# A Fourier mixing layer with a gated product: the inverse's butterflies leave VectorE, two products of a step trade places, and a slot moves

## The chip, the cores and the metric

The kernel runs on one core of a Trainium2 chip. The metric is device time in microseconds, the median of three executions. The five engines run their own queues in order: PE (TensorE, matmuls), DVE (VectorE), ACT (ScalarE), POOL (GpSimd) and SP (which issues DMAs). An instruction that waits holds up all behind it on its engine.

## What is computed

For 8 batches of 3072 tokens of 256 features: a Fourier transform along the tokens, a complex 256 x 256 mixing with bias, a soft threshold, the inverse transform, and on its real output y a gated product of three weight matrices:

```
X  = rfft(x, axis=1)
Yr = Xr @ w_r - Xi @ w_i + b_r ;  Yi = Xr @ w_i + Xi @ w_r + b_i
Y  = soft(Yr) + 1j * soft(Yi)        # sign(a) * max(|a| - 0.01, 0)
y  = irfft(Y, n=3072, axis=1)
out = ((y @ w_a) * (y @ w_b)) @ w_out   # 256 -> 1536 -> 256
```

## The kernel before

The tokens are cut into 32 pairs of blocks (4 pairs a batch, 2 x 384 tokens each). The gated product of a pair runs in 12 steps, one for each 128 columns of the 1536, so there are 384 steps in a row; they are named pair.step here (5.3 is step 3 of pair 5). The step is in `step`. The two products with w_a and w_b are done as seven products of 384 columns, `run(0)` to `run(5)` in the step itself and a seventh, run(6), in `last_prod` one step later. Each is split into high and low parts, so each is three matmuls: ych with the low weight (wcNl), ych with the high one (wcNh), ycl with the high one. The result of a step, g, is multiplied with w_out in four pieces, `proj` 0 to 3, one step later; a piece too is three matmuls (0 and 1 of 256 columns, 2 and 3 of 512).

A step works in two of the PSUM banks X (bank_75 and bank_76 by turns) and in ya (bank_77) and yb (bank_78). ACT copies X after run(0) (the copy s1) and after run(2) (s2), and yb after run(3) (s5), since the next product is added on top or a later operation needs the part alone. run(2) needs s1 done, run(4) needs s5, run(5) needs s2. After run(4) a chain of four makes g from yb: two DVE products, a cast on ACT, a subtraction on DVE; run(3) of the next step needs yb, proj 0 and 1 need g. After run(5) DVE adds X to s5, and run(6) needs that. After run(6) a chain of three makes the other half of g, for proj 2 and 3.

Between the products a step has two slots. `slot()` takes a task from a list: a piece of the transform of the next batch. f1 is the first stage; f2 reads gs (sums on POOL); f3 has two halves, of which the second ends with four reads of its bank by DVE (the tile zy); i1 is the inverse's first stage, stored to d_d. All tasks share one bank, bank_79, so a task waits until the one before has been read.

The inverse's last stage is done by no matmul but by sums and scalings in SBUF: `idft` loads a tile wk from d_d and does some thirty operations on it in one chain, the last four of which write y. `yr_sums` follows with three sums of y on DVE, `yr_split` with the high and low parts (ych on ACT, ycl on POOL or DVE), into a ring. All this must be there when the next pair starts; in the last step of a pair, `yr_have` puts out whatever is missing, ahead of the rest of the step.

The order of the instructions on each engine is made by the class `Order`, a planner that keeps its own clock (`pe`, moved on by each matmul) and for each engine the time at which it comes free. `chain` gives it operations, each with the engines that may take it (G is POOL, V DVE, A ACT). Urgent ones go out when they are ready; `lazy` ones when they could start by now; `spare` ones after the lazy ones. Between two operations on different engines it reckons `HOP` = 165 ns. While `hold` is set, lazy and spare operations on ACT that would end after it are kept back. `need` puts a chain out and moves the planner's clock to its end, `vacate` the same for a bank.

Of the kernel before, what the change touches and what calls it, by code (L numbers as in the profile page):

```python
# [15 lines left out]
ALU = mybir.AluOpType  # L16

B, S, D, DFF = 8, 3072, 256, 1536
# [191 lines left out]
class Order:  # L210
# [35 lines left out]
    def chain(self, *ops, urgent=0, spare=False, after=0.0):  # L246

        c = {"ops": deque(ops), "left": len(ops), "n": len(ops), "times": [(max(self.pe + self.FROM, after), None)], "urgent": urgent}  # L250
        if urgent:
            self._push(c)
        else:
            (self.spare if spare else self.lazy).append(c)
        return c

    def _ready(self, c, engine=None):
        op = c["ops"][0]
        back = min(op[3] if len(op) > 3 else 1, len(c["times"]))
        t, e = c["times"][-back]  # L260
        return t if e is None else t + (self.same if e == (engine or op[0][0].upper()) else self.HOP)
# [99 lines left out]
def fft_mix_glu_kernel(ctx: ExitStack, tc: tile.TileContext, x, w_r, w_i, b_r, b_i, w_a, w_b, w_out, c1f, vf, m2, t2, c3, b1, m2b, vb, out):  # L361
# [24 lines left out]
    def tt(e, o, a, b, op):  # L386
        (nc.vector if e == "V" else nc.gpsimd).tensor_tensor(o, a, b, op=op)  # L387
# [675 lines left out]
    C3, C8, T8 = math.sqrt(0.75), math.cos(math.pi / 8), math.tan(math.pi / 8)  # L1063
    HALF = math.sqrt(0.5)

    def idft(b, q, wait=False):
# [14 lines left out]
        def size(*dims):  # L1081
            return math.prod(n for _, n in dims) * (1 if dims[-1][0] == 1 else 16)

        def add(o, x, y, op=ALU.add, engines="GV", back=1):
            n = size(*o[1:])
            o, x, y = (z if isinstance(z, bass.AP) else at(*z) for z in (o, x, y))
            ops.append((engines, n, lambda e: tt(e, o, x, y, op), back))

        def sub(o, x, y, **kw):
            add(o, x, y, ALU.subtract, **kw)  # L1090
# [6 lines left out]
        def mul_add(o, x, f, y, op=ALU.add):  # L1097
            n = size(*o[1:])
            o, x, y = at(*o), at(*x), at(*y)
            ops.append(("V", n, lambda e: nc.vector.scalar_tensor_tensor(o, x, f, y, op0=ALU.mult, op1=op)))  # L1100

        rows, flat = ((W, 4), (1, P)), ((1, 512),)
        x = [(A + P * i, *rows) for i in range(3)]
        sub((T, (P, 4), (1, P)), x[1], x[2])
# [3 lines left out]
        mul_add(x[2], x[1], -0.5, x[0])  # L1108
        add(x[0], x[0], x[1])
        turn = (640, (P, 4), (1, P))  # L1110
# [6 lines left out]
        for r, f in ((slice(0, 3, 2), C8), (slice(1, 2), HALF)):  # L1117
            v = (T2 + 192 * r.start, (384, 2), (1, 192)) if r.start == 0 else (T2 + 192, (1, 192))
            scale(v, v, f)
        o = [[(T2 + 192 * r + 16 * c, (32, 6)) for c in range(2)] for r in range(3)]  # L1120
        w = [[(A + 192 * r + 16 * c, (32, 6)) for c in range(2)] for r in range(3)]
        mul_add(w[0][0], o[0][1], T8, o[0][0])
        mul_add(w[0][1], o[0][0], -T8, o[0][1])
        mul_add(w[2][0], o[2][0], T8, o[2][1], ALU.subtract)
        mul_add(w[2][1], o[2][1], T8, o[2][0])
# [29 lines left out]
        for th in range(2):  # L1155
            for pq in range(2):
# [3 lines left out]
                ops.append(("GV", W, last))  # L1160
        yr["idft"] = od.chain(*ops, ("S", 0, lambda e: yr_sums(p)), after=ready)
# [125 lines left out]
    def step(n, nxt):  # L1287
# [27 lines left out]
        od.vacate(X)  # L1315
        run(0, X, True)
# [15 lines left out]
        od.need(c1_)  # L1332
        run(2, X)
# [5 lines left out]
        if not (tasks and tasks[0]):  # L1339
            od.hold = od.pe + 3 * (W / 2.4 + 2.8) + od.FROM  # L1340
# [5 lines left out]
        proj(pp, pj, 0)  # L1346
        slot()
        if n == 0:
            busy(3, *unread)
        proj(pp, pj, 1)  # L1350
        od.need(c5_)
        od.hold = None
# [15 lines left out]
        od.need(c2_)  # L1368
        run(5, X)
        od.put(c5_)  # L1370
        held[p, j] = X, s5, od.chain(add(s5, X), urgent=1)
        for i in range(2, 4):
            proj(pp, pj, i)
# [229 lines left out]
```

## Time and profile before

| | us |
|---|---|
| median of 3 executions (lowest, highest) | 2836.59 (2834.68, 2836.78) |
| the profiled execution | 2837.05 |
| its span, first to last instruction | 2835.3 |
| PE busy | 2792.2 (98%) |
| DVE busy | 2006.7 (71%) |
| ACT busy | 1397.7 (49%) |
| POOL busy | 1300.4 (46%) |
| mean granted clock of PE | 0.999 of full speed |

Matmuls overlap in the profile: the next one starts 0.17 us after a 384-column one whose own row says 0.34. So a busy PE can still lose time, and the distance from start to start tells more than the busy share. A product of three without a wait takes 0.52 us.

### The profile page before, as it was taken

What the parts mean: (1) busy time and instruction counts of PE and PEld (TensorE: products, weight loads), DVE (VectorE), ACT (ScalarE), POOL (GpSimd) and SP (SyncE); (2) the same over time, 40 slices, a digit from 0 to 9 for tenths busy, and PEclk for the clock granted to TensorE, in tenths of its full rate; (3) what the DMA queues carried; (4) which work ended last, traced back from release to release, by engine and by line L of the source; (5) the groups of instructions that cost most, each with busy time, mean ns of one, the idle gap of its engine ahead of it and who ended that gap; (6) DMA issues with size and microseconds to landing.
All of it is one profiled execution on the core that took longest, in us unless ns stands there. A gap on an engine that the chain in (4) does not pass through costs nothing.

```text
span 2835.3 us, 46772 instructions
## 1 busy us (share of the span) xinstructions
PE 2792.2 (98%) x16375; PEld 2605.7 (92%) x16375; DVE 2006.7 (71%) x3801; ACT 1397.7 (49%) x3059; POOL 1300.4 (46%) x1466
## 2 busy tenths in 40 slices
PE   9999999999999999999999999999999999999999
PEld 6799998999999999999999999999999999999998
DVE  4876667777677776777766777668677677666665
ACT  4654445544455444644446444464444544444443
POOL 1233336456364453654545644356544566343330
PEclk9999999999999999999999999999999999999999
DMA  8531113212132111321113121131211322110000
GB/s 248 169 101 48 54 53 100 82 44 62 54 93 71 57 49 50 100 69 56 48 46 114 60 68 33 59 105 54 68 36 56 109 62 67 37 39 21 22 8 23
DMA packets 157056, 190.91 MB, mean 67 GB/s; under 512 B 28344, under 2 KB 117300, under 8 KB 156740
## 3 DMA queue, kind: packets, MB, share of 16 engines
q1 hardware_dynamic: 154620, 180.12, 20.7%
q0 software_dynamic: 2000, 7.61, 0.9%
q8 instruction: 128, 2.10, 0.3%
q14 instruction: 108, 0.88, 0.1%
q10 hardware_dynamic: 200, 0.20, 0.0%
HBM read 112.03 MB, written 75.71 MB: 66 GB/s over the span
## 4 chain that ended last, share of the span: by engine, by line
PE 88%; DVE 4%; ACT 3%; issue 2%; DMA 2%; POOL 1%; SPq 0%; ACTq 0%; DVEq 0%; POOLq 0%
PE bank L393 88%; DVE bank L387 1%; DVE s L387 1%; ACT s L1305 1%; POOL wk L387 1%; ACT wk L1095 1%; DMA xin<-in_x_dram 1%; ACT g L1362 0%; ACT dst L384 0%; ACT gst L384 0%; DMA g_d<-gst 0%; DVE x L387 0%; DMA d_d<-dst 0%; DMA wraw<-in_moe_w_a_dram 0%; ACT osb L384 0%
## 5 line engine op out<-in xcount | busy, mean ns | idle before, releaser
L387 DVE TENSOR_TENSOR bank<-bank,s 128x384 f32<-128x384 f32 x1152 | 648.5, 563 | 430.4 <-PE bank L393 410.7
L1305 ACT COPY s<-bank 128x384 f32<-128x384 f32 x1152 | 545.0, 485 | 199.3 <-PE bank L393 195.8
L1362 ACT CAST g<-bank 128x384 fp32r<-128x384 f32 x384 | 184.2, 480 | 819.7 <-DVE s L387 462.7
L387 POOL TENSOR_TENSOR wk<-wk 128x96 f32<-128x96 f32 (+4 forms) x562 | 444.0, 810 | 234.0 <-DMA wk<-d_d 120.0
L387 DVE TENSOR_TENSOR g<-bank,g 128x384 fp32r<-128x384 f32 x768 | 425.9, 556 | 170.8 <-ACT g L1362 155.0
L387 DVE TENSOR_TENSOR s<-bank,s 128x384 f32<-128x384 f32 x768 | 423.3, 551 | 10.0 <-PE bank L393 0.4
L387 POOL TENSOR_TENSOR zh<-zy,zc 128x512 f32<-128x512 f32 x84 | 114.9, 1367 | 612.6 <-DVE zc L955 450.4
L1280 ACT CAST g<-bank 128x384 fp32r<-128x384 f32 x384 | 184.5, 480 | 245.8 <-DVE bank L387 244.0
L393 PE MATMUL bank<-ych,wc1l 128*128 128x384 f32 x672 | 236.3, 352 | 4.1 <-DVE s L387 2.1
L393 PE MATMUL bank<-ych,wc3l 128*128 128x384 f32 x672 | 236.6, 352 | 2.8 <-ACT s L1305 2.7
L393 PE MATMUL bank<-ych,wc2l 128*128 128x384 f32 x672 | 236.0, 351 | 1.8 <-ACT s L1305 1.8
L393 PE MATMUL bank<-ych,wc0l 128*128 128x384 f32 x672 | 236.2, 351 | 0.9 <-ACT s L1305 0.5
L393 PE MATMUL bank<-ycl,wc0h 128*128 128x384 f32 x672 | 226.8, 337 | 0.9 <-DVE ycl L387 0.9
L393 PE MATMUL bank<-ycl,wc3h 128*128 128x384 f32 x672 | 226.8, 338 | 0.0
L393 PE MATMUL bank<-ycl,wc2h 128*128 128x384 f32 x672 | 226.8, 338 | 0.0
L393 PE MATMUL bank<-ycl,wc1h 128*128 128x384 f32 x672 | 226.8, 338 | 0.0
L393 PE MATMUL bank<-ych,wc1h 128*128 128x384 f32 x672 | 226.8, 338 | 0.0
L393 PE MATMUL bank<-ych,wc2h 128*128 128x384 f32 x672 | 226.8, 337 | 0.0
L393 PE MATMUL bank<-ych,wc0h 128*128 128x384 f32 x672 | 226.6, 337 | 0.0
L393 PE MATMUL bank<-ych,wc3h 128*128 128x384 f32 x672 | 226.1, 337 | 0.0
L393 PE MATMUL bank<-wm_h,sx 128*128 128x256 f32 x1008 | 186.9, 282 | 0.0
L387 POOL TENSOR_TENSOR ycl<-y,ych 128x384 fp32r<-128x384 f32 x138 | 148.6, 1091 | 72.4 <-ACT ych L509 71.8
(208 smaller groups left out, 6583.0 us busy)
## 6 DMA issues: line engine op xcount, KB each, us to landing
d_d<-dst SPq DMA_DIRECT2D x96, 256.0 KB
out_dram<-osb SPq DMA_DIRECT2D x64, 384.0 KB
g_d<-gst SPq DMA_DIRECT2D x91, 240.0 KB
wk<-d_d SPq DMA_DIRECT2D x28, 768.0 KB
xin<-in_x_dram SPq DMA_DIRECT2D x107, 192.0 KB
gt<-g_d SPq DMA_DIRECT2D x154, 128.0 KB
vt<-const_vb_dram SPq DMA_DIRECT2D x91, 128.0 KB
m_in<-const_m2b_dram SPq DMA_DIRECT2D x84, 128.0 KB
```

The lines of the kernel that those rows point to most:

```text
L387: (nc.vector if e == "V" else nc.gpsimd).tensor_tensor(o, a, b, op=op)
L393: nc.tensor.matmul(o, lhsT=l, rhs=r, start=start, stop=stop, **kw)
L1095: ops.append(("A", n, lambda e: nc.scalar.mul(o, x, f)))
L1280: ("A", W, lambda e: nc.scalar.copy(h, X)),
L1305: return s, od.chain(("A", W, lambda e: nc.scalar.copy(s, q[:, :W])), urgent=1)
L1362: ("A", W, lambda e: nc.scalar.copy(h1, Y)),
```

## The change

Three things are changed. In `idft`, every sum and difference may go to POOL alone (before: POOL, or DVE where that would end much sooner), and the combined multiply-and-add operations, which only DVE has, are written as a scaling on ACT and a sum on POOL. The chain becomes a spare one, and the planner reckons 800 ns instead of 165 between two of its operations on different engines. In `step`, run(5) now comes ahead of run(4); the second slot moves from between proj 0 and 1 to between proj 2 and 3. `hold` is now set ahead of run(0) where the first slot is empty, until run(2), and ahead of run(3) always, until run(5); before, it was set ahead of run(3) alone, where the second slot was empty, until run(4).

```diff
@@ -243,11 +243,11 @@
             self.pe = min(t, self.pe + 250.0)
             self.flush()
-    def chain(self, *ops, urgent=0, spare=False, after=0.0):
-        c = {"ops": deque(ops), "left": len(ops), "n": len(ops), "times": [(max(self.pe + self.FROM, after), None)], "urgent": urgent}
+    def chain(self, *ops, urgent=0, spare=False, after=0.0, hop=None):
+        c = {"ops": deque(ops), "left": len(ops), "n": len(ops), "times": [(max(self.pe + self.FROM, after), None)], "urgent": urgent, "hop": self.HOP if hop is None else hop}
         if urgent:
             self._push(c)
         else:
@@ -258,7 +258,7 @@
         op = c["ops"][0]
         back = min(op[3] if len(op) > 3 else 1, len(c["times"]))
         t, e = c["times"][-back]
-        return t if e is None else t + (self.same if e == (engine or op[0][0].upper()) else self.HOP)
+        return t if e is None else t + (self.same if e == (engine or op[0][0].upper()) else c["hop"])
     def _push(self, c):
         self.count += 1
@@ -1060,7 +1060,7 @@
         od.reads(bk, c, len(then))
         yr[th, dh] = c
-    C3, C8, T8 = math.sqrt(0.75), math.cos(math.pi / 8), math.tan(math.pi / 8)
+    C3, C8, S8 = math.sqrt(0.75), math.cos(math.pi / 8), math.sin(math.pi / 8)
     HALF = math.sqrt(0.5)
     def idft(b, q, wait=False):
@@ -1081,48 +1081,43 @@
         def size(*dims):
             return math.prod(n for _, n in dims) * (1 if dims[-1][0] == 1 else 16)
-        def add(o, x, y, op=ALU.add, engines="GV", back=1):
+        def add(o, x, y, op=ALU.add):
             n = size(*o[1:])
             o, x, y = (z if isinstance(z, bass.AP) else at(*z) for z in (o, x, y))
-            ops.append((engines, n, lambda e: tt(e, o, x, y, op), back))
-        def sub(o, x, y, **kw):
-            add(o, x, y, ALU.subtract, **kw)
+            ops.append(("G", n, lambda e: tt(e, o, x, y, op)))
+        def sub(o, x, y):
+            add(o, x, y, ALU.subtract)
         def scale(o, x, f):
             n = size(*o[1:])
             o, x = at(*o), at(*x)
             ops.append(("A", n, lambda e: nc.scalar.mul(o, x, f)))
-        def mul_add(o, x, f, y, op=ALU.add):
-            n = size(*o[1:])
-            o, x, y = at(*o), at(*x), at(*y)
-            ops.append(("V", n, lambda e: nc.vector.scalar_tensor_tensor(o, x, f, y, op0=ALU.mult, op1=op)))
-        rows, flat = ((W, 4), (1, P)), ((1, 512),)
+        rows = ((W, 4), (1, P))
         x = [(A + P * i, *rows) for i in range(3)]
-        sub((T, (P, 4), (1, P)), x[1], x[2])
+        half, turn = ((o, (P, 4), (1, P)) for o in (T, 640))
+        sub(half, x[1], x[2])
         add(x[1], x[1], x[2])
         scale((640, (32, 16)), (T + 16, (32, 16)), -C3)
         scale((656, (32, 16)), (T, (32, 16)), C3)
-        mul_add(x[2], x[1], -0.5, x[0])
+        scale(half, x[1], -0.5)
+        add(x[2], x[0], half)
         add(x[0], x[0], x[1])
-        turn = (640, (P, 4), (1, P))
         add(x[1], x[2], turn)
         sub(x[2], x[2], turn)
         bp, bq = ((A + N2 * i, (P, 9), (1, N2)) for i in range(2))
         sub((T2, (N2, 9), (1, N2)), bp, bq)
         add((T, (N2, 9), (1, N2)), bp, bq)
-        for r, f in ((slice(0, 3, 2), C8), (slice(1, 2), HALF)):
-            v = (T2 + 192 * r.start, (384, 2), (1, 192)) if r.start == 0 else (T2 + 192, (1, 192))
-            scale(v, v, f)
-        o = [[(T2 + 192 * r + 16 * c, (32, 6)) for c in range(2)] for r in range(3)]
-        w = [[(A + 192 * r + 16 * c, (32, 6)) for c in range(2)] for r in range(3)]
-        mul_add(w[0][0], o[0][1], T8, o[0][0])
-        mul_add(w[0][1], o[0][0], -T8, o[0][1])
-        mul_add(w[2][0], o[2][0], T8, o[2][1], ALU.subtract)
-        mul_add(w[2][1], o[2][1], T8, o[2][0])
+        outer, mid, sine = (T2, (384, 2), (1, 192)), (T2 + 192, (1, 192)), (A + 576, (192, 2), (1, 192))
+        scale(sine, outer, S8)
+        scale(outer, outer, C8)
+        scale(mid, mid, HALF)
+        o, si, w = ([[(b + 192 * r + 16 * c, (32, 6)) for c in range(2)] for r in range(3)] for b in (T2, A + 576, A))
+        add((A, (400, 2), (32, 6)), (T2, (384, 2), (32, 6)), (A + 576 + 16, (192, 2), (32, 6)))
+        sub(w[0][1], o[0][1], si[0][0])
+        sub(w[2][0], si[1][0], o[2][1])
         add(w[1][0], o[1][0], o[1][1])
         sub(w[1][1], o[1][1], o[1][0])
@@ -1157,8 +1152,8 @@
                 def last(e, th=th, pq=pq):
                     y = yr["tile"][:, (2 * th + pq) * W : (2 * th + pq + 1) * W].rearrange("p (s n) -> p s n", s=2)
                     tt(e, y, at(*far(T + 192 + 192 * pq)), at(*(far(T) if pq else near(R0))), ALU.subtract if th else ALU.add)
-                ops.append(("GV", W, last))
-        yr["idft"] = od.chain(*ops, ("S", 0, lambda e: yr_sums(p)), after=ready)
+                ops.append(("G", W, last))
+        yr["idft"] = od.chain(*ops, ("S", 0, lambda e: yr_sums(p)), after=ready, spare=True, hop=800.0)
     def yr_sums(p):
         a11, a12, a21, a22 = yr["y"]
@@ -1313,6 +1308,8 @@
             out_weights(n - 3 + EARLY)
         X = x_ps[n % 2]
         od.vacate(X)
+        if not (tasks and tasks[0]):
+            od.hold = od.pe + 3 * (W / 2.4 + 2.8) + od.FROM
         run(0, X, True)
         s1, c1_ = take(X)
         if n:
@@ -1330,26 +1327,29 @@
         if n == 0:
             busy(3, *unread)
         od.need(c1_)
+        od.hold = None
         run(2, X)
         s2, c2_ = take(X)
         if n == 0:
             od.put(c2_)
             yr_split(0, 5, 3)
         od.vacate(yb)
-        if not (tasks and tasks[0]):
-            od.hold = od.pe + 3 * (W / 2.4 + 2.8) + od.FROM
+        od.hold = od.pe + 3 * (W / 2.4 + 2.8) + od.FROM
         run(3, yb, True)
         s5, c5_ = take(yb)
         if n == 0:
             od.put(c5_)
             yr_split(0, 6, 3)
-        proj(pp, pj, 0)
-        slot()
+        for i in range(2):
+            proj(pp, pj, i)
         if n == 0:
             busy(3, *unread)
-        proj(pp, pj, 1)
+        od.need(c2_)
+        od.hold = None
+        run(5, X)
+        od.put(c5_)
+        held[p, j] = X, s5, od.chain(add(s5, X), urgent=1)
         od.need(c5_)
-        od.hold = None
         run(4, yb)
         if n:
             od.put(gs[pp, pj][3])
@@ -1365,12 +1365,9 @@
         )
         od.reads(yb, c, 0)
         gs[p, j] = [h, l, c, None]
-        od.need(c2_)
-        run(5, X)
-        od.put(c5_)
-        held[p, j] = X, s5, od.chain(add(s5, X), urgent=1)
-        for i in range(2, 4):
-            proj(pp, pj, i)
+        proj(pp, pj, 2)
+        slot()
+        proj(pp, pj, 3)
         gs.pop((pp, pj), None)
     def f1_tasks(b):
```

On PE, in step 3 of pair 5, before: proj 0 and 1 (bank_73), between them the task of slot 2, an f2 (m_in,gs into bank_79); then run(4) into yb (bank_78) and run(5) into X (bank_76).

```order
L393 MATMUL bank_73<-g,wo2l 128x256
L393 MATMUL bank_73<-g,wo2h 128x256 x2
L393 MATMUL bank_79<-m_in,gs 128x2x64 x4
L393 MATMUL bank_73<-g,wo2l 128x256
L393 MATMUL bank_73<-g,wo2h 128x256 x2
L393 MATMUL bank_78<-ych,wc1l 128x384
L393 MATMUL bank_78<-ych,wc1h 128x384
L393 MATMUL bank_78<-ycl,wc1h 128x384
L393 MATMUL bank_76<-ych,wc1l 128x384
L393 MATMUL bank_76<-ych,wc1h 128x384
L393 MATMUL bank_76<-ycl,wc1h 128x384
```

The same place of the changed kernel, from proj 1 on:

```order
L393 MATMUL bank_73<-g,wo2l 128x256
L393 MATMUL bank_73<-g,wo2h 128x256 x2
L393 MATMUL bank_76<-ych,wc1l 128x384
L393 MATMUL bank_76<-ych,wc1h 128x384
L393 MATMUL bank_76<-ycl,wc1h 128x384
L393 MATMUL bank_78<-ych,wc1l 128x384
L393 MATMUL bank_78<-ych,wc1h 128x384
L393 MATMUL bank_78<-ycl,wc1h 128x384
L393 MATMUL bank_72<-g,wo2l 128x512
L393 MATMUL bank_72<-g,wo2h 128x512 x2
L393 MATMUL bank_79<-m_in,gs 128x2x64 x4
```

run(5) stands ahead of run(4), and the task comes after proj 2 (bank_72).

On DVE, at the end of pair 3, before: from the end of step 3.10 into the last step, 3.11. The operations on bank_75 to 78 are the steps' own (g<-bank_78 is the subtraction that ends the chain on yb); s_4504, y and s_4505 are the three sums on y for pair 4, ycl the low parts for the ring.

```order
L387 TENSOR_TENSOR bank_78<-bank_78,s 128x384 x2
L387 TENSOR_TENSOR s<-bank_75,s 128x384
L387 TENSOR_TENSOR g<-bank_78,g 128x384
L387 TENSOR_TENSOR s_4504<-y 128x384
L387 TENSOR_TENSOR y<-y 128x12x32
L387 TENSOR_TENSOR s_4505<-y 128x384
L387 TENSOR_TENSOR bank_75<-bank_75,s 128x384
L387 TENSOR_TENSOR s<-bank_77,s 128x384
L387 TENSOR_TENSOR ycl<-y,ych 128x384
L387 TENSOR_TENSOR g<-bank_75,g 128x384
```

The same place of the changed kernel:

```order
L387 TENSOR_TENSOR s<-bank_75,s 128x384
L387 TENSOR_TENSOR bank_78<-bank_78,s 128x384 x2
L387 TENSOR_TENSOR s_4504<-y 128x384
L387 TENSOR_TENSOR y<-y 128x12x32
L387 TENSOR_TENSOR s_4505<-y 128x384
L387 TENSOR_TENSOR bank_75<-bank_75,s 128x384
L387 TENSOR_TENSOR s<-bank_77,s 128x384
L387 TENSOR_TENSOR ycl<-y,ych 128x384
L387 TENSOR_TENSOR g<-bank_78,g 128x384
L387 TENSOR_TENSOR g<-bank_75,g 128x384
```

The subtraction from bank_78 that stood ahead of the three sums now stands behind them, behind two operations of the step and a low part.

On DVE, at the end of pair 7, before: steps 7.9 to 7.11, with the sums s_8060, y and s_8061 for pair 8.

```order
L387 TENSOR_TENSOR s_8060<-y 128x384
L387 TENSOR_TENSOR y<-y 128x12x32
L387 TENSOR_TENSOR bank_78<-bank_78,s 128x384
L387 TENSOR_TENSOR s<-bank_76,s 128x384
L387 TENSOR_TENSOR bank_78<-bank_78,s 128x384
L387 TENSOR_TENSOR s_8061<-y 128x384
L387 TENSOR_TENSOR g<-bank_78,g 128x384
L387 TENSOR_TENSOR bank_76<-bank_76,s 128x384
L387 TENSOR_TENSOR s<-bank_77,s 128x384
L387 TENSOR_TENSOR g<-bank_76,g 128x384
L387 TENSOR_TENSOR bank_78<-bank_78,s 128x384 x2
L387 TENSOR_TENSOR s<-bank_75,s 128x384
```

The same place of the changed kernel, with the sums s_8138, y and s_8139:

```order
L387 TENSOR_TENSOR s<-bank_75,s 128x384
L387 TENSOR_TENSOR bank_78<-bank_78,s 128x384 x2
L387 TENSOR_TENSOR s_8138<-y 128x384
L387 TENSOR_TENSOR y<-y 128x12x32
L387 TENSOR_TENSOR s_8139<-y 128x384
L387 TENSOR_TENSOR bank_75<-bank_75,s 128x384
L387 TENSOR_TENSOR s<-bank_77,s 128x384
L387 TENSOR_TENSOR g<-bank_78,g 128x384
L387 TENSOR_TENSOR g<-bank_75,g 128x384
```

The sums, which were spread among the operations of two steps, stand in one row ahead of the last step's own, and the subtraction from bank_78 is behind them.

## Rows read from the trace of the kernel before

**Rows 1.** The page, part 1: busy time, share of the span, instructions.

```profile
span 2835.3 us, 46772 instructions
...
PE 2792.2 (98%) x16375; PEld 2605.7 (92%) x16375; DVE 2006.7 (71%) x3801; ACT 1397.7 (49%) x3059; POOL 1300.4 (46%) x1466
```

**Rows 2.** Groups of PE: operation, tiles, shape, count | busy us, mean ns | idle before.

```profile
L393 PE MATMUL bank<-ych,wc3l 128*128 128x384 f32 x672 | 236.6, 352 | 2.8 <-ACT s L1305 2.7
...
L393 PE MATMUL bank<-ych,wc3h 128*128 128x384 f32 x672 | 226.1, 337 | 0.0
```

**Rows 3.** Timeline, step 29.9, PE and ACT: start us, us, operation, [idle before].

```profile
2668.40 0.33 PE L393 MATMUL bank<-ych,wc3l 128*128 128x384 f32 x1
...
2668.92 0.28 PE L393 MATMUL bank<-g,wo8l 128*128 128x256 f32 x1
...
2669.65 0.45 PE L393 MATMUL bank<-ych,wc3l 128*128 128x384 f32 x1
2669.93 0.34 PE L393 MATMUL bank<-ych,wc3h 128*128 128x384 f32 x1
...
2670.83 0.39 PE L393 MATMUL bank<-g,wo8l 128*128 128x512 f32 x1
...
2672.22 0.34 PE L393 MATMUL bank<-ych,wc3l 128*128 128x384 f32 x1
...
2668.65 0.94 ACT L1305 COPY s<-bank 128x384 f32<-128x384 f32 x2
```

**Rows 4.** Timeline of PE: first and last of 212 late starts of run(4).

```profile
122.15 0.45 PE L393 MATMUL bank<-ych,wc0l 128*128 128x384 f32 x1
...
2818.48 0.45 PE L393 MATMUL bank<-ych,wc3l 128*128 128x384 f32 x1
```

**Rows 5.** Timeline, PE and DVE, slot 2: the first of 53 waits, step 5.3, the last.

```profile
144.00 0.72 PE L393 MATMUL bank<-x,c_sb 120*120 120x512 f32 x2 [1.56 <-ACT gst L384]
...
576.51 0.34 PE L393 MATMUL bank<-ych,wc1l 128*128 128x384 f32 x1
...
577.67 0.40 PE L393 MATMUL bank<-g,wo2h 128*128 128x256 f32 x2
578.54 1.13 PE L393 MATMUL bank<-m_in,gs 128*128 128x128 f32 x8 [0.47 <-POOL wk L387]
...
577.58 0.86 DVE L387 TENSOR_TENSOR zy<-bank,k 64x256 f32<-64x256 f32 x2
...
2455.00 1.13 PE L393 MATMUL bank<-m_in,gs 128*128 128x128 f32 x8 [0.54 <-issue]
```

**Rows 6.** Waits of PE's weight loads: who for whom, us, times, longest.

```profile
PEld bank L393 <- DVE s L387: 6.2, 13, 0.5
```

**Rows 7.** Timeline, end of pair 3: the inverse's tail on ACT, POOL, DVE; PE's wait.

```profile
452.20 0.53 ACT L1095 ACTIVATE wk<-wk 128x384 f32<-128x384 f32 x1
...
452.80 3.22 POOL L387 TENSOR_TENSOR wk<-wk 128x192 f32<-128x192 f32 x4 [2.88 <-ACT wk L1095]
456.10 3.94 POOL L387 TENSOR_TENSOR y<-wk 128x384 f32<-128x384 f32 x4
...
460.08 1.35 DVE L387 TENSOR_TENSOR s<-y 128x384 f32<-128x384 f32 x1 [1.26 <-POOL y L387]
461.46 0.56 DVE L387 TENSOR_TENSOR y<-y 128x384 f32<-128x384 f32 x1
...
463.97 0.45 PE L393 MATMUL bank<-ych,wc3l 128*128 128x384 f32 x1 [2.73 <-ACT s L1305]
```

**Rows 8.** Groups of POOL, ACT and DVE, each shape apart; columns as in rows 2.

```profile
L387 POOL TENSOR_TENSOR wk<-wk 128x512 f32<-128x512 f32 x128 | 170.2, 1330 | 171.5 <-DMA wk<-d_d 120.0 <-DVE wk L1100 39.9 <-ACT s L1305 6.1
...
L384 ACT COPY osb<-bank 128x512 f32<-128x512 f32 x64 | 39.1, 612 | 0.7 <-PE bank L393 0.6
...
L387 DVE TENSOR_TENSOR y<-wk 128x384 f32<-128x384 f32 x36 | 36.7, 1059 | 0.0
```

**Rows 9.** Busy time by stretch, us; then PE's granted clock, DMA share, GB/s.

```profile
140.00:150.00 10.00, 8.44 (x36) 7.30 (x36) 7.92 (x15) 4.26 (x10) 5.28 (x4) 0.83 0.46 134
```

## What the change will do to the time: the prediction

> **What bounds the kernel now.** I read the first part of the page, then the groups of TensorE, then stretches of the timeline. The span is 2835.3 us, TensorE is busy for 2792.2 of it, no other engine for more than 2007 [rows 1]. So only TensorE's own waiting can be won, and DVE, ACT and GpSimd count only where TensorE waits for them. Its waits show in two ways. One is the plain gaps, 43 us in all. The other is hidden in the busy time: a product is three matmuls, and the first of them takes 352 ns, the second 337 [rows 2]. That is 236.6 - 226.1 = 10.5 us in this group of 672, and there are four such groups: some 40 us are lost by first matmuls that got their weights late.
>
> To see where, I set the starts of neighbouring matmuls against each other. In a step without side work, run(3) starts at 2668.40, ACT starts its two copies s2 and s5 at 2668.65 and ends at 2669.59, and run(4), which writes into the bank that s5 empties, starts at 2669.65. Its second matmul starts 0.28 later, where 0.17 to 0.18 is usual [rows 3]: some 0.1 lost. Between run(3) and run(4) lie only proj 0 and 1, from 2668.92 on, 0.71 us when nothing waits; s5's copy ends 0.67 after run(3) does, and the weight load comes ahead of the matmul. From first to last [rows 4] this occurs 212 times with 0.105 on average (22.2 us), and 33 more times there is a longer gap ahead of run(4) (10.2 us): **32.4 us at run(4)**.
>
> The second place is the second slot. There is one spare bank, so a task must wait until the task before it has been read out. In step 3 of pair 5, the product behind f3's second half starts at 576.51, DVE's four reads end at 578.44, and f2's first matmul follows at 578.54, though proj 0's last two started at 577.67 [rows 5]: 0.63 lost. From first to last [rows 5] there are 53 such waits behind proj 0, 27.0 us, and 4.9 on the matmuls right behind them: **31.9 us at slot 2**. The first, 1.7 us at 142.2, is an input that is not ready; I leave it in, which makes 30.2.
>
> Third, run(6) waits 13 times for DVE's sum into s5, 6.2 us [rows 6]. The other late firsts (most at run(2), where ACT's copy is not the cause) and the waits of run(3) for its bank, some 5 us, I leave in.
>
> **The change part by part.** *The swap.* Between run(3) and run(4) now stand proj 0, proj 1 and run(5): 0.71 + 0.52 = 1.23 us, for a need of 0.67 and a weight load ahead (0.85 at most) [rows 3]. run(5) needs s2 only, whose copy ends half a microsecond before s5's, and has 0.52 + 0.71 = 1.23 too. So the 32.4 us at run(4) go in every step where ACT is on time, and run(5) takes over none. The sum into s5 comes 0.5 us earlier relative to run(6), so its 6.2 go as well. What is later: the four-operation chain behind run(4) starts 0.52 later and must be done by run(3) and proj 0 of the next step. It needs about 2.6 us from run(4)'s end (two DVE products, an ACT cast, a DVE subtraction, 0.5 to 0.6 each with 0.1 to 0.2 between), and proj 2 and 3 (2670.83 to 2672.22, 1.38) and four products of 0.52 lie there, 3.5 us [rows 3]. Covered, with 0.9 to spare.
>
> *The slot.* Slot 1 to slot 2 was 1.4 us of TensorE work (run(2), run(3), proj 0) and becomes 3.5. Slot 2 to the next slot 1 was 4.3 and becomes proj 3, run(0), run(6), run(1), 0.69 + 1.57 = 2.26. The longest readout takes 2.03 from the end of the task to the release, 576.51 to 578.54 [rows 5]. So the 30.2 us go. About 24 times in the run f2 now meets f3's four reads across the short side, where nothing is to spare: 0 to 0.6 each, I take 0.1, **+2.4**.
>
> *The inverse.* 230 DVE operations leave (146 us in 7 groups, the largest but one 36 at 1059 ns), GpSimd gets 202 more, at most 1.33 us each [rows 8], 270 us at the very most on 1300. ACT gets 56, some 30 us. None of it is on TensorE's path while the inverse is done in time. In the order the four y of a pair's inverse stand in step 5 to 9 of the pair before (3 to 8 before the change), and TensorE needs them in step 11. There are two exceptions.
>
> First, **pair 3 to 4**. The order puts the inverse's last ACT scale into step 11 itself, and behind it on GpSimd four sums and the four y. In the trace of before that tail took from 452.20 to 460.04, 7.85 us [rows 7], and was ahead by one step. DVE's three sums (1.35 and twice 0.56) need all four y, and in the new order they, two bank operations and one ring subtraction stand ahead of the subtraction that frees run(3)'s bank. From run(0)'s start: scale at 0.5, y done at 8.3, DVE through at 12.9; run(3) would be due at 2.1. That is **10.9 us**. Before, the same place cost 2.9 (the wait at 463.97), which is in the 32.4 already.
>
> A pause like that can lower TensorE's clock. In this trace the stretch from 140 to 150, with the 1.7 us pause in it, has a mean of 0.83 of full speed [rows 9], so 10 x 0.17 = **1.7 us** of work at the full level are lost to the lower one; I add that once, though the pause of 2.9 at 461 left the clock full. The Trainium skill (TensorE: Matmul & The Clock Gate, Part 1) has the clock fall to 1.2 GHz after an idle stretch and rise again when busy; by it the fall is near certain here, and its price would be the same.
>
> Second, **the last step of pairs 7, 11, ..., 27**. There the three sums on y were spread over steps 9 and 10 and now stand in one row ahead of run(3)'s subtraction: 3 x 0.5 us later, of which about 0.45 is covered. 6 x (1.05 + 0.2 at run(4)) = **7.5 us**.
>
> *ACT.* In one step near the start and one at the end of each of 12 middle pairs, the order has four or five ACT operations of 0.4 to 0.6 [rows 8] between s1 and s2, where one to three stood. s2 is then about 1 us late, and run(5) has 0.5 to spare (1.23 less 0.25 from run(2)'s end to the copy and 0.47 for it [rows 3]): 24 x 0.3 = **7.2 us**, between 0 and 24 x 0.6. The end of the program loses a proj's wait, **0.5**.
>
> The rule that speaks against moving sums to GpSimd is in the Trainium skill (SBUF — State Buffer, Who interferes with whom): a DVE instruction with two SBUF inputs and a GpSimd instruction that reads SBUF exclude each other. The trace agrees: the first sum took 1.35 us beside a GpSimd subtraction, the next, of the same shape, 0.56 [rows 7]. The operations that TensorE waits for read one operand from PSUM, so by the rule it would add at most 0.8 at each of the 7 places above, 6 us, and the time would be 2804.
>
> **The sum.** Removed 32.4 + 30.2 + 6.2 = 68.8. Added 2.4 + 10.9 + 1.7 + 7.5 + 7.2 + 0.5 = 30.2. Net 38.6. The profiled execution took 2837.05 us, 1.75 more than its span and 0.5 above the median of 2836.59, so no correction: **2798 us**.
>
> **The rivals.** *A, only the certain price is paid:* ACT's pile-ups and the short slot cost nothing, and run(3)'s 5 us go too: 2837 - 68.8 - 5 + 10.9 + 1.7 = 2776. For it: slack of 0.5 us or more at each of those places; against it: my walk through the order finds ACT behind in just these steps. *B, the waits move and stay:* run(5) is late as run(4) was, 212 x 0.1 = 21, and the short slot costs 24 x 0.6 = 14 instead of 2.4: 2798 + 21 + 12 = 2831. For it: s2 and s5 are copied in one go [rows 3], and a late s2 hits run(5) first. Against it: s2 ends 0.47 before s5, with the same cover. *C, slower, the inverse comes too late:* GpSimd is one queue, the inverse is now behind everything in it. If the first inverse of a batch slips so far that its y end in step 11, each of the 6 further batches pays what pair 3 pays, 6 x 10.9 = 65: 2863. It decides at about 8 us of slip, since the y stand in step 9. For it: 202 more GpSimd operations and a chain with no second engine. Against it: these 6 inverses run where GpSimd is idle for most of the time, and at 30 operations each the extra is 5 to 9 us over some 30, with the order's own allowance for it.
>
> **How the numbers follow.** Forecast 0.55 (2784 to 2815 with its bounds on ACT), A 0.25 (2768 to 2784), B 0.11 (2815 to 2838), C 0.09 (over 2840). Less than 0.2% (5.7 us) is about what a measurement of this kernel cannot tell from no change. A and the forecast are faster, half of B is (to 2831): faster 0.86; the other half of B is the same: 0.06; C with a rest: slower 0.08. For 8 in 10 I go from 2770, in the middle of A, to 2824.
>
> **What would show it.** Right: the wcNl groups near 344 ns instead of 352; DVE near 1860 us busy, GpSimd near 1470; no gap between proj 0 and proj 1; one pause of about 11 us near 460 us ahead of run(3), with y and the three sums in front of it. Wrong: late first matmuls at run(5) (B); GpSimd's y after step 10 at 800, 1150, 1490 us (C); no pause at pair 3 (my walk was wrong, and the time nearer A).

## The result and the profile after

The changed kernel took **2791.3 us** (2789.7 to 2792.0) against 2836.7 for the kernel before, 0.984 of its time with a 95% interval of 0.9823 to 0.9858: 45.4 us less. The forecast was 2798, with 2770 to 2824 around it. The profiled execution has a span of 2789.3 us, 46.0 less than in [rows 1].

The page of the changed kernel, part 1, and two of the groups of TensorE (columns as in [rows 1, 2]):

```profile
span 2789.3 us, 45735 instructions
...
PE 2752.6 (99%) x16375; PEld 2594.3 (93%) x16375; DVE 1910.6 (68%) x3595; ACT 1425.6 (51%) x3115; POOL 1413.0 (51%) x1644
...
L393 PE MATMUL bank<-ych,wc3l 128*128 128x384 f32 x672 | 233.3, 347 | 16.9 <-DVE g L387 14.3
...
L393 PE MATMUL bank<-ych,wc3h 128*128 128x384 f32 x672 | 226.4, 337 | 0.0
```

The first matmuls fell from 352 to 347 ns in this group and to 341 to 343 in the other three: fewer of them get their weights late. But the group now also has 16.9 us of plain gaps ahead of it, 14.3 of them put down to DVE, where it had 2.8. Both readings have a place in the program.

Step 29.9 again, run(3), proj 0, proj 1, run(5), run(4), from the timelines of PE and ACT (answers to [rows 3]):

```profile
2626.30 0.33 PE L393 MATMUL bank<-ych,wc3l 128*128 128x384 f32 x1
...
2627.17 0.28 PE L393 MATMUL bank<-g,wo8l 128*128 128x256 f32 x1
...
2627.53 0.34 PE L393 MATMUL bank<-ych,wc3l 128*128 128x384 f32 x1
2627.70 0.34 PE L393 MATMUL bank<-ych,wc3h 128*128 128x384 f32 x1
...
2628.06 0.35 PE L393 MATMUL bank<-ych,wc3l 128*128 128x384 f32 x1
2628.24 0.34 PE L393 MATMUL bank<-ych,wc3h 128*128 128x384 f32 x1
...
2626.55 0.94 ACT L1300 COPY s<-bank 128x384 f32<-128x384 f32 x2
```

ACT still copies s2 and s5 in one go, from 2626.55 to 2627.49. Yet the second matmul of run(5) starts 0.17 after its first, and that of run(4) 0.18 after its own, where 0.28 stood in [rows 3]. A whole pair of the last batch shows what this makes: from the first run(0) of pair 29 to that of pair 30 TensorE took 71.80 us before and takes 69.31 now.

The pause that the prediction looked for near 460 us, from the timelines of PE, ACT, POOL and DVE, and two stretches with the granted clock (columns as in [rows 9]):

```profile
469.17 0.69 PE L393 MATMUL bank<-ych,wc3l 128*128 128x384 f32 x1 [9.59 <-DVE g L387]
...
457.77 0.53 ACT L1095 ACTIVATE wk<-wk 128x384 f32<-128x384 f32 x1
...
458.37 3.18 POOL L387 TENSOR_TENSOR wk<-wk 128x192 f32<-128x192 f32 x4 [1.92 <-ACT wk L1095]
461.63 3.85 POOL L387 TENSOR_TENSOR y<-wk 128x384 f32<-128x384 f32 x4
...
465.51 0.56 DVE L387 TENSOR_TENSOR s<-y 128x384 f32<-128x384 f32 x1 [8.23 <-POOL y L387]
...
468.57 1.01 DVE L387 TENSOR_TENSOR g<-bank,g 128x384 fp32r<-128x384 f32 x2
...
460.00:470.00 10.00, 0.83 (x3) 0.83 (x4) 4.42 (x10) 2.60 (x6) 5.32 (x6) 0.70 0.31 102
470.00:475.00 5.00, 5.00 (x19) 4.72 (x18) 3.25 (x8) 1.82 (x4) 1.00 (x1) 0.57 0.01 3
```

One reads it from below: run(3) waits for g's subtraction, which frees its bank; that stands on DVE behind three sums on y; they wait for the four y on GpSimd; those for the last ACT scale. After it TensorE runs at the lower level of its clock until about 474.

Two smaller waits, in the last step of pair 7 (run(3), six such places) and of pair 5 (run(5), 14 such places), from the timelines of PE and ACT:

```profile
809.87 0.44 PE L393 MATMUL bank<-ych,wc3l 128*128 128x384 f32 x1 [0.79 <-DVE g L387]
...
645.75 0.45 PE L393 MATMUL bank<-ych,wc3l 128*128 128x384 f32 x1
...
644.72 0.59 ACT L384 COPY dst<-bank 128x512 f32<-128x512 f32 x1
645.20 0.88 ACT L1300 COPY s<-bank 128x384 f32<-128x384 f32 x2
```

### The profile page after: what moved, and what is told of

It reads as the page before. It is cut to its first block, busy times and chain, and to the rows that moved or that the text cites. A ratio compares the mean times of both kernels' runs of the same rounds, so it can differ in the third digit from the quotient of the medians.

```text
span 2789.3 us, 45735 instructions
## 1 busy us (share of the span) xinstructions
PE 2752.6 (99%) x16375; PEld 2594.3 (93%) x16375; DVE 1910.6 (68%) x3595; ACT 1425.6 (51%) x3115; POOL 1413.0 (51%) x1644
## 3 DMA queue, kind: packets, MB, share of 16 engines
q1 hardware_dynamic: 154620, 180.12, 21.2%
## 4 chain that ended last, share of the span: by engine, by line
PE 92%; DVE 3%; ACT 3%; DMA 1%; issue 1%; POOL 0%; SPq 0%; ACTq 0%; DVEq 0%; POOLq 0%
PE bank L393 92%; DVE s L387 1%; DVE bank L387 1%; DMA xin<-in_x_dram 1%; ACT s L1300 0%; ACT ych L509 0%; ACT g L1362 0%; DVE g L387 0%; DVE y L387 0%; DMA d_d<-dst 0%; ACT dst L384 0%; ACT sx L807 0%; ACT xs L384 0%; ACT g L1275 0%; SPq L640 0%
## 5 line engine op out<-in xcount | busy, mean ns | idle before, releaser
L387 POOL TENSOR_TENSOR wk<-wk 128x96 f32<-128x96 f32 (+4 forms) x728 | 565.8, 800 | 231.6 <-DMA wk<-d_d 116.0
L387 POOL TENSOR_TENSOR zh<-zy,zc 128x512 f32<-128x512 f32 x84 | 108.6, 1293 | 478.1 <-PE bank L393 314.1
L393 PE MATMUL bank<-ych,wc3l 128*128 128x384 f32 x672 | 233.3, 347 | 16.9 <-DVE g L387 14.3
L393 PE MATMUL bank<-ych,wc2l 128*128 128x384 f32 x672 | 230.2, 343 | 2.1 <-ACT s L1300 2.0
L393 PE MATMUL bank<-ych,wc1l 128*128 128x384 f32 x672 | 230.1, 342 | 1.4 <-DVE g L387 0.7
L393 PE MATMUL bank<-ych,wc0l 128*128 128x384 f32 x672 | 229.4, 341 | 0.1
L387 POOL TENSOR_TENSOR ycl<-y,ych 128x384 fp32r<-128x384 f32 x115 | 120.1, 1060 | 126.3 <-ACT ych L509 126.3
```

Source lines behind the costliest of these rows:

```text
L393: nc.tensor.matmul(o, lhsT=l, rhs=r, start=start, stop=stop, **kw)
```

## The experiments

All times are medians; since the kernel before gave 2836.4 to 2838.4 in the four groups of runs, kernels are compared by their difference from the before of their own group. "Late" sums are counted as in the prediction: the distance between the starts of neighbouring matmuls, less the usual one of its kind.

| kernel | us | against before |
|---|---|---|
| swap alone | 2817.4 | -20.0 (0.9930, 0.9915 to 0.9945) |
| slot alone | 2880.6 | +43.2 (1.0153, 1.0136 to 1.0170) |
| inverse alone | 2830.2 | -7.3 (0.9972, 0.9961 to 0.9984) |
| swap, slot and holds | 2809.1 | -28.4 (0.9900, 0.9885 to 0.9914) |
| the same, and the inverse's place in the order | 2791.0 | -47.4 (0.9833, 0.9819 to 0.9848) |
| swap, slot, holds, and the inverse's engines | 2806.3 | -32.0 (0.9885, 0.9870 to 0.9900) |
| the full change | 2791.3 | -45.4 (0.9840, 0.9823 to 0.9858) |

**The swap alone.**

```
 proj 0, slot 2, proj 1
-run(4, yb) ... run(5, X)
+run(5, X) ... run(4, yb)
 proj 2, proj 3
```

> The swap alone: run(5) and run(4) trade places, slot 2 stays between proj 0 and proj 1, the inverse stays on three engines. My theory: the 32.4 us of late starts at run(4) and the 6.2 at run(6) go, nothing takes their place, slot 2 keeps its 31.9: 2836.6 - 38.6 = 2798 us, run(4) and run(5) both without late first matmuls. Rival (the waits only move): s2 and s5 are copied in one go, so run(5) is late as run(4) was, 212 x 0.1 = 21 us stay: 2819 us.

Measured: 20 us, half of it. The waits at run(4) and run(6) are gone as expected, but run(3), which was late by 5.2 us in all, is now late by 24.8 (5.4 of it in the last step of pair 3, whose pause stood at run(4) before). The time is near the rival's, but by chance: its mechanism did not come, run(5) is late by 0.9 us in all. One place where run(3) waits, pair 7, step 5, from the timelines of DVE and PE:

```profile
771.48 1.59 DVE L387 TENSOR_TENSOR wk<-wk 128x512 f32<-128x512 f32 x1
772.99 0.68 DVE L387 TENSOR_TENSOR x<-xin,x 120x512 fp32r<-120x512 f32 x1
...
774.52 0.54 DVE L387 TENSOR_TENSOR g<-bank,g 128x384 fp32r<-128x384 f32 x1
...
775.12 0.44 PE L393 MATMUL bank<-ych,wc1l 128*128 128x384 f32 x1 [1.29 <-DVE g L387]
```

An inverse sum and the low half of a transform input stand on DVE ahead of the four operations that follow run(4). With run(4) half a microsecond later, there is no room for them any more.

**The slot alone.**

```
-proj 0, slot 2, proj 1, run(4), run(5), proj 2, proj 3
+proj 0, proj 1, run(4), run(5), proj 2, slot 2, proj 3
```

> The slot alone: slot 2 between proj 2 and proj 3, run(4) ahead of run(5) as before, the inverse on three engines. Plain sum: the 30 us at slot 2 go: 2807 us. My theory: the two are not independent. A task between proj 0 and proj 1 covered ACT's copy of s5, which is why only 245 of 382 steps were late at run(4); with the task gone from there the other 137 are late too, 137 x 0.105 = 14 us: 2821 us, and the count of late run(4) near 370. Rival (the short side between slot 2 and the next slot 1 costs 0.6 in 24 steps): 14 us more, at slot 1.

Measured: 43 us slower. The waits behind proj 0 are gone, and run(4) is late in every step, as the theory had it (40.6 us instead of 22.2). Its miss is the size: the gaps ahead of run(4), 10.2 us before, are 54.9 now. The waits of the weight loads, before and in this kernel (who for whom: us, times, longest):

```profile
PEld bank L393 <- ACT s L1305: 15.0, 39, 2.9
```

```profile
PEld bank L393 <- ACT s L1305: 70.4, 119, 2.9
```

A task between proj 0 and proj 1 had not only covered ACT's usual copy, but ACT's late ones too. So the slot pays only together with the swap.

**The inverse alone.**

```
 before's step, products and slots
+idft: sums on GpSimd, scales on ScalarE; spare=True, hop=800.0; holds
```

> The inverse alone: all its sums on GpSimd, its scales on ACT, its later place in the order and the holds, with the step's products and slots as before. My theory: it only costs. The pause at the end of pair 3 grows from 2.9 to about 10 (+7), the clock behind it +2.4, the last step of six pairs +6, ACT's pile-ups in 24 steps hit run(4), which has 0.5 less cover than run(5) in the full change, +13; nothing is gained but the 6.2 at run(6) at most: 2859 to 2865 us. Rival (VectorE is what the late steps wait for, and 230 fewer operations on it pay): 2820 us or less.

Measured: 7 us faster; the theory falls. The costs that it names are there: ahead of run(4) 19.4 us, with one gap of 7.9 at pair 3 and six of 1.45. But of 53 waits at slot 2 only 24 are left (12 each in steps 3 and 10), 13.1 us less with the matmuls right behind them, and the late starts at run(6) and run(3) fall by 8.5. The inverse's part also takes something away.

**Swap and slot, with the holds, without the inverse's part.**

```
-idft: sums on GpSimd, scales on ScalarE; spare=True, hop=800.0
+idft as before
```

> Swap and slot together with the holds of the full change, the inverse on three engines as before. My theory: 32.4 + 30.2 + 6.2 go, and what the inverse's move adds (some 27 us: pause at pair 3, clock, six last steps, ACT's pile-ups) is not there: 2836.6 - 68.8 = 2768 us, up to 2774 if the short pause near 461 us stays and moves to run(3). Rival (the relief of VectorE is what lets the other two parts pay): 2791 us or more.

Measured: 2809, and the rival is right: the inverse's part brings another 17 us. Late here are run(3) by 27.2 us (33 times), run(5) by 17.5 (38 times), and the last third of proj 2, with what follows, by 7.2 (13 times, 12 of them in step 5). Of the waits at run(3), 6.0 us are a pause at pair 3, so that pause is there without the inverse's part too. So are 14 late run(5) in last steps, 6.0 us, the same 14 as in the full change. The one of pair 5, from ACT's timeline, to be set beside the lines at 644.72 and 645.20 above:

```profile
643.65 0.60 ACT L384 COPY dst<-bank 128x512 f32<-128x512 f32 x1
644.13 0.88 ACT L1305 COPY s<-bank 128x384 f32<-128x384 f32 x2
```

In this place, as in the 11 others at the end of a middle pair, the same copy of a task's bank, dst, stands ahead of s2 in both kernels, and no scale of the inverse.

**The engines and the place apart.** The two halves of the inverse's part: the engines its sums may use, and its chain's place in the order (behind the transform work, with the long hop).

```
 swap, slot, holds
-idft: GpSimd and VectorE
+idft: GpSimd and VectorE; spare=True, hop=800.0        (order only)
+idft: GpSimd alone, scales on ScalarE; place as before (engines only)
```

> Swap, slot and holds, with the inverse still on three engines (VectorE too) but its chain behind the transform work and with the long hop. It parts two things that the change does to the inverse: the engines and the place in the order. Theory E (the engines): in the run without the inverse's part run(3) waited 23.5 us for a bank that VectorE frees late, because the inverse's sums stand in VectorE's queue; they still do here, so the time stays near 2809, 2803 to 2812 us. Theory P (the place): the later place alone keeps the sums from the steps in which VectorE is short; the time falls to 2791 to 2797 us.

> The full change with the inverse on GpSimd and ScalarE alone, but its chain at the old place in the order (not behind the transform work, no long hop). Theory E: VectorE is free of the inverse, so the waits at run(3) are gone as in the full change; the pause at pair 3 shrinks, since the y end half a step earlier (step 3.10 to 3.11, not inside 3.11); ACT's scales stand earlier and may delay s1 and s2: 2783 to 2791 us. Theory P: without the later place the waits come back: 2800 us or more.

Measured: the place gives all of it (-47.4), the engines alone 4 us of 17 (-32.0). By the times measured, Theory P holds and E falls. But one half of E holds: with the engines alone run(3) is on time. Outside pair 3 and the last steps it is late by 21.2 us in the kernel with swap and slot, by 6.0 with the place and by 2.3 with the engines. What the engines win there they lose elsewhere: run(5) is late by 19.0 us instead of 17.5, run(2) by 8.3 instead of 1.9, and proj 2 in step 2 by 9.7. The waits of TensorE, swap and slot first, then with the engines (who for whom: us, times, longest):

```profile
PE bank L393 <- DVE g L387: 20.9, 22, 5.5
PE bank L393 <- ACT s L1305: 6.4, 14, 1.0
```

```profile
PE bank L393 <- DVE g L387: 19.1, 10, 7.4
PE bank L393 <- ACT s L1300: 11.3, 31, 1.0
```

What moved shows in one group of DVE, each shape apart, the low halves of the transform inputs. First swap and slot, then with the place, then with the engines:

```profile
L387 DVE TENSOR_TENSOR x<-xin,x 120x512 fp32r<-120x512 f32 x32 | 37.0, 1155 | 32.8 <-ACT x L509 32.8
```

```profile
L387 DVE TENSOR_TENSOR x<-xin,x 120x512 fp32r<-120x512 f32 x2 | 1.4, 686 | 0.4 <-ACT x L509 0.4
```

```profile
L387 DVE TENSOR_TENSOR x<-xin,x 120x512 fp32r<-120x512 f32 x20 | 22.1, 1103 | 19.1 <-ACT x L509 19.1
```

Of 91 such subtractions the order gives some to VectorE, 2 to 37 in the kernels of this document (15 in the kernel before, 14 in the full change), according to how full it holds GpSimd's queue to be when they come. What one of them does, in the kernel with the engines alone (pair 8, step 2; timelines of DVE and PE):

```profile
832.80 1.62 DVE L387 TENSOR_TENSOR x<-xin,x 120x512 fp32r<-120x512 f32 x1 [1.80 <-ACT x L509]
...
834.81 0.54 DVE L387 TENSOR_TENSOR g<-bank,g 128x384 fp32r<-128x384 f32 x1
...
835.41 0.50 PE L393 MATMUL bank<-g,wo0h 128*128 128x512 f32 x1 [1.44 <-DVE g L387]
```

DVE waits 1.8 us for ACT's half of the input, then takes 1.62 for its own, and g's low half, which proj 2's third matmul needs, is behind it. Six batches have this place, 1.6 us each.

**The transform inputs on GpSimd.** Swap and slot as above, the inverse as before, and one line:

```
-od.chain(*split(512, xi, xh, xl), after=t)
+od.chain(*split(512, xi, xh, xl, "G" if b > 1 else "GV"), after=t)
```

> Swap, slot and holds with the inverse on three engines at its old place (2809 us), and one thing more: from batch 2 on the low half of each transform input (the subtraction x<-xin,x) is put on GpSimd always, where the order had left 30 of them to VectorE. It asks by which way the inverse's place in the order acts. Theory X: an inverse that stands ahead of the transform work fills GpSimd's queue, the order then gives these subtractions (1.1 us each) to VectorE, and they stand ahead of the operations that free run(3)'s bank and proj 2's operand; with them gone the waits at run(3) in steps 2 and 4 (about 8 us with the late matmuls behind) and at proj 2 in step 5 (5 us) go: 2796 us, 2792 to 2799. Theory S: it is the inverse's own sums on VectorE and its scales on ACT; nothing changes: 2806 to 2811 us.

Measured: 2792.5, -44.0 (0.9841, 0.9827 to 0.9856) where -28.4 stood. Theory X holds for run(3), which is late by 8.7 us instead of 27.2. One detail of it is wrong: the waits at proj 2 in step 5 stayed (7.1 us), and so did those at run(5) (18.0 us). So this one line gives nearly the time of the inverse's whole part, but not by the same sum: the full change also takes 10.6 us off run(5) and clears proj 2 in step 5, and pays for it with a longer pause at pair 3 (10.1 us instead of 6.0), the last step of six pairs (6.4) and run(2). The later place thus acts in a second way that the transform inputs do not explain.

**The hold.** The full change without the hold between run(0) and run(2).

> The full change without the new hold between run(0) and run(2) (the one ahead of run(3) stays). If the hold is what keeps ACT's copy s1 on time, run(2) is late more often: 12 waits at run(2) become 30 or more of about 0.4, +7 to +12: 2798 to 2803 us. If the order leaves ACT's queue nearly the same without it, no change: 2791 us, within 3.

Measured: 2791.3, -47.1 (0.9831, 0.9815 to 0.9848). This hold does nothing here.

**The pause at pair 3.** Two of the next batch's tasks go into empty slots of pair 1; then also the first inverse of each batch gets the ordinary hop; then also the transform inputs go to GpSimd.

```
-work += [None] * 2 + mids[:3] + [None] + mids[3:11] + fin + mids[11:17]
+work += [None] + mids[:11] + fin + mids[11:19]
-hop=800.0
+hop=800.0 if q else None
```

> The full change with one thing moved: two of the next batch's middle tasks go from pair 3 into two empty slots of pair 1, so that the inverse of pair 4 starts one step earlier and its y end in step 3.10. My theory: the pause of 9.8 us ahead of run(3) near 459 us falls to 4 or less and the slow clock behind it goes: 2791.3 - 6 - 2.4 = 2783 us, 2780 to 2786. Rival (the pause comes from somewhere else, such as the DMA that brings the inverse's input): the pause stays and the time with it, 2791 us.

> The full change with the inverse of each batch's first pair given the ordinary hop (its y end half a step earlier) and, in pair 1, the two middle tasks moved up as in the run before. What is left of the pause at pair 3 (4.7 us) and the 0.95 us ahead of run(3) in the last step of six pairs should go, if they come from y that end too late and from three sums in one row: 2787.1 - 4.7 - 6 x 1.05 = 2776 us, 2775 to 2779. Rival: ACT's scales, now earlier too, delay s1 and s2 in the steps before, 7 batches x 3 scales x 0.3 = 6: 2782 us.

> The run before this one, with the transform inputs' subtraction on GpSimd always from batch 2 on as well (14 of them stood on VectorE in the full change). Theory X: a few of the remaining waits go, 3 us at most: 2773 to 2776 us. Rival: GpSimd's queue gets longer by 12 x 1.3 us and the subtraction is late for its own product: 2780 us or more.

Measured: 2787.1, 2779.3 and **2775.2** (-51.3, -57.2, -61.2; the last 0.9782 of before, 0.9767 to 0.9796, and faster than both kernels); the first two lie 1.1 and 0.3 us above the ranges expected, the third in its own. The wait ahead of run(3) near 460 us in the first two, from the timeline of PE:

```profile
467.69 0.69 PE L393 MATMUL bank<-ych,wc3l 128*128 128x384 f32 x1 [4.53 <-DVE g L387]
```

```profile
463.08 0.44 PE L393 MATMUL bank<-ych,wc3l 128*128 128x384 f32 x1 [1.16 <-DVE g L387]
```

The pause went as y came earlier, so its cause is the late y. The first run gave 4 to 6 us where 8 were expected: its matmul still takes 0.69, the lower clock, and a task of pair 1 now waits 1.1 for its input. In the second the clock stayed, and the six waits in last steps are gone; ACT took back some 3 us at run(2). In the third the transform subtractions on GpSimd gave 4 more.

**The named part undone.** The fastest kernel with the inverse's sums back on VectorE and GpSimd.

> The run before (2775.2 us) with the one part undone that the change is named for: the inverse's sums back on VectorE and GpSimd, everything else (swap, slot, holds, place, the first inverse's earlier start, transform subtractions on GpSimd) as there. Theory N (taking the inverse off VectorE is worth nothing by itself): 2772 to 2778 us, within 0.1%. Theory E (it is worth what the comparison without the place showed, 2809.1 - 2806.3 = 3 us, or more): 2778 to 2785 us, with new waits at run(3) in steps 1 and at run(5) in step 4.

Measured: 2776.0, 0.9787 of before (0.9774 to 0.9801) against 0.9782. VectorE is busy for 1980 us there and for 1901 in the fastest kernel. Theory N holds: once the place and the transform inputs are as they are there, it is worth nothing to take the inverse off VectorE. At the old place it was worth some 4 us, little more than the spread of the runs.

## Why the prediction was right, and where its reasons were not

By its own terms, each counted in the two traces in the same way:

| term | predicted | measured |
|---|---|---|
| run(4) | -32.4 | -32.3 |
| slot 2 | -30.2 | -29.5 |
| run(6) | -6.2 | -5.8 |
| f2 across the short side | +2.4 | +0.2 |
| pause at pair 3 | +10.9 | +9.9 |
| clock behind it | +1.7 | +2.6 |
| last step of six pairs | +7.5 | +6.4 |
| ACT's pile-ups | +7.2 | +10.0 |
| run(3) elsewhere | 0 | -3.2 |
| gaps under 0.05 ahead of run(4) | 0 | -4.5 |
| end and the rest | +0.5 | +0.2 |
| sum | -38.6 | -46.0 (span) |

*The swap and the slot.* The three removed terms are right to a microsecond here. Of the 53 waits behind proj 0 none is left; in their place is one of 2.05 at 138.6, in pair 0. The short side costs nothing.

*The pause.* It is where the walk through the order put it, and for that reason; 9.9 lost instead of 10.9. Not all of it is the inverse's: the kernel with swap and slot alone loses 6.0 there. The y were done 8.2 us after run(0)'s start (8.3 in the sum), but the first sum on y took 0.56 where [rows 7] had 1.35, so DVE was through in 3.5 us and not in 4.6. The clock: 5 x (1 - 0.57) = 2.2 from 470 to 475 and half of 0.83 ahead of that. The wait of 2.1 us at 138 has its own 1.6 us of low clock (0.84 from 140 to 150), as the one at 142 had before. The rule on the port that DVE and GpSimd share (the Trainium skill, SBUF — State Buffer, Who interferes with whom), which would have added 0.8 at each of seven places, added nothing there: GpSimd stood idle beside the three sums, at pair 3 and in the six last steps, and each took 0.55 to 0.56.

*The six last steps.* 0.95 and 0.11 each, 1.06 instead of 1.25.

*ACT.* The term that was mis-sized: 6.8 us at run(5), nearly all of it in step 11, and 3.2 more than before at run(2), in steps 5 and 8. That the sum is near is luck in part: the late run(5) of step 11 are there without the inverse's part too, behind the copy of a task's bank. The pile-ups at the start of the middle pairs did not hurt here; they do in the kernel with swap and slot alone (12 at run(5) in step 1, 12 in step 4).

*What was left out.* Of the 5.2 us at run(3) that the forecast kept and rival A took off, 3.2 went, and with the swap went 4.5 us of gaps of less than 0.05 each between proj 1 and run(4), which my count had not seen. Together they are the difference between 2798 and 2791; the other misses cancel. Of A's other conditions one held (the slot) and one did not (ACT). B did not come: run(5) is late by 0.6 us in all outside last steps. C did not come: the first inverse's y of pair 7 start at 800.2 us, in step 9, as ordered.

*The signs.* DVE is busy for 1911 us, not 1860, and GpSimd for 1413, not 1470: 31 more splits of y fell to VectorE than before (24 us), and its sums of the transform's copies (xq<-xs) went from 24 in 16 us to 35 in 45 us. The prediction had counted neither.

**What was wrong is a reason, not the number.** The prediction credits the swap and the slot with 68.8 us and charges the inverse with 27. The runs show that swap and slot alone (with the holds) give 28, and that the inverse's part brings 17. The late starts that the swap and the slot remove are gone there too, but others stand in their place: 27.2 us at run(3), 17.5 at run(5), 7.2 at proj 2. The inverse's part takes much of these away. The step that fails is the one on the chain behind run(4), "covered, with 0.9 to spare". It was read from a step without side work. In steps with transform work one subtraction of 0.7 to 1.6 us, or one inverse sum, on VectorE uses up the 0.9, and run(3) waits.

In the full change VectorE is clear in nearly all of these steps, so the sum came out; as far as it rests on that step this was luck, for the prediction had no term for what clears them. Three things do, each by itself: the inverse's chain behind the transform work, the inverse off VectorE, and the transform's subtractions held on GpSimd. The first is worth the 17 us, with the inverse still on VectorE; the second only some 4, since late starts at proj 2, run(5) and run(2) come in place of those at run(3); the third, 15.6. What links the first and the third is a thing that the prediction did not count: an operation that may go to either of two engines moves when the queue of one is modelled as longer.

What stays open: why the late starts at slot 2 in steps 1, 2, 4 and 5 go with the inverse's part alone was not taken apart further. The inverse on two engines at its old place, with the transform inputs held on GpSimd, was not tried. The hold ahead of run(3) was never taken out by itself, so what it adds to the 28.4 us of swap, slot and holds is not known. Nor is it shown by which way the later place clears run(5) and proj 2.

## What to carry to other kernels

A cover that is read from a quiet step holds for quiet steps only: before the end of a chain is moved later, list what else stands on its engine in the busiest step. Where an order may choose between two engines, moving one chain moves others that the diff does not name; comparing counts of each kind of operation per engine, before and after, shows them. And two moves that each look like a gain can need each other: the slot alone cost 43 us; the swap alone gave 20, and both, with the holds, 28.

## What the runs showed of the hardware

Two operations of VectorE stretched several times over beside GpSimd, and TensorE waited for them. Pair 0, step 3 of the changed kernel, timelines of POOL, DVE and PE:

```profile
133.34 1.85 POOL L387 TENSOR_TENSOR wc3l<-w,wc3h 128x768 fp32r<-128x768 f32 x1 [0.34 <-ACT wc3h L509]
135.68 1.82 POOL L387 TENSOR_TENSOR wc3l<-w,wc3h 128x768 fp32r<-128x768 f32 x1 [0.49 <-ACT wc3h L509]
...
133.42 1.92 DVE L499 TENSOR_SCALAR wo_a<-wo_a 128x256 f32<-128x256 f32 x1
...
135.71 2.07 DVE L501 SCALAR_TENSOR_TENSOR wo_a<-wo_raw,wo_a 128x256 uint32<-128x256 uint32 x1
...
144.23 0.28 DVE L499 TENSOR_SCALAR wo_a<-wo_a 128x256 f32<-128x256 f32 x1
...
138.63 0.50 PE L393 MATMUL bank<-g,wo2h 128*128 128x512 f32 x1 [2.05 <-DVE g L387]
```

The same TENSOR_SCALAR takes 0.28 us at 144.23; at 133.42 it takes 1.92, and ends 0.15 behind a subtraction of GpSimd that began 0.08 ahead of it. The SCALAR_TENSOR_TENSOR at 135.71 began 0.03 behind the next one and ended 0.28 behind it. The Trainium skill (SBUF — State Buffer, Who interferes with whom) says of a VectorE instruction in a mode that uses both ports that whoever issues first gets the shared pair of ports for the whole instruction, and the other is blocked; it has a VectorE instruction with two inputs in SBUF contend with GpSimd's reads too. The times agree at both places; in which mode the TENSOR_SCALAR ran, the trace does not show.

The traces do not bear out that the length of a pause alone decides whether the clock falls. In the changed kernel (columns as in [rows 9]):

```profile
140.00:150.00 10.00, 10.00 (x48) 9.22 (x47) 7.62 (x15) 6.02 (x13) 3.94 (x4) 0.84 0.53 152
```

After 2.05 us ahead of 138.6 the granted clock was 0.84 from 140 to 150; after 4.53 ahead of 467.7, in the run with two tasks moved, the next matmul took 0.69; after 1.16 ahead of 463.1, in the run after that, and, in the kernel before, 2.73 ahead of 463.97 [rows 7] it took 0.44 and 0.45.
